# Thirty tiny loads in two groups in a single-token attention and MLP kernel

## The chip, the cores and the metric

The kernel runs on one core of one Trainium2 chip. The metric is the device time of one execution in microseconds. The kernel before was timed three times: 193.33, 193.45 and 193.55 us, median 193.45 us.

## The reference: what is computed

One token `x` (512 numbers) goes through a layer norm, and then through two branches.

```python
xn = _layernorm(x, axis=-1)
s = _A_ref(xn, A_k_cache, A_v_cache, A_wq, A_wo)   # attention
g = _silu(_B_ref(xn, B_w1, B_w2, B_w3, B_w4))      # MLP
return x + s * g
# in _A_ref: 32 heads of 128; the last W = 4096 of 32768 cached positions
q = x @ wq
scores = einsum(q, k) * 128 ** -0.5;  p = softmax(scores);  o = einsum(p, v) @ wo
# in _B_ref: x1 = x + shifted(h) @ w2;  h2 = gelu(layernorm(x1) @ w3) @ w4;  return x1 + h2
```

With one token, the four shifts of the MLP push all of `h` out, so `w1` is never needed, and the kernel multiplies `w2` with zeros. The bulk of the data is 32 heads x 4096 positions x 128 numbers of 2 bytes, once for K and once for V: 67 MB of the 79 MB that the kernel moves.

## The kernel before, in words

**Groups and stages.** The 32 heads are taken four at a time: eight groups, each with one K tile and one V tile of 4 MB (`load_kv`). The main loop (line 531) has ten passes `s`; in pass `s` the keys of group `s` are scored and the values of group `h = s - 2` are used. Below, K3 is the K tile of group 3, V0 the V tile of group 0. K0 comes in two transfers of 2 MB, K0a and K0b; V7 in three, V7a (2 MB), V7b and V7c (1 MB each). K has three buffers, V two. The two V buffers lie in the memory of the pool `wts`, which holds the weights `wq`, `w2`, `w3`, `w4` and what is made from them; the pool is closed in pass 2, so V0 is issued only once everything that reads this pool is done.

**Who does what.** For each group VectorE (DVE) multiplies a part of the keys with the query and sums along the row (`k_vector`, lines 321 and 323, in four parts); the other part is transposed on TensorE (PE), copied by ScalarE (ACT, line 342) and scored on PE (line 350). `sm_max`, `sm_turn`, `sm_exp`, `sm_den` and `sm_rden` make the softmax; `v_wide` (line 427) multiplies with the values. The query row is made on PE from `wq` (line 208); ACT and DVE copy it to `q_row` (lines 210, 211), ACT copies it once more (line 218), and spreads it over the partitions as `q_bc` (line 216), which every product of line 321 needs. Then ACT writes `q_pair` (line 225), which the scores on PE need.

**The order of the work.** From line 527 on, PE, DVE and ACT follow the order written out by hand in the loop. Ahead of it, a scheduler places the instructions. Loads go through two queues: SP issues the weights `w2`, `w3`, `w4` (its last 96 rows as a transfer of their own, "the tail of w4"), all K and V tiles, the `wo` tiles and the store, in the order of the program (`load`, line 75). ACT issues `x_bf`, `x_row` and `wq` (lines 79 to 84), in line with its other instructions.

**Completion counters.** A transfer raises a counter when it lands. In the built program there are eight of these counters, and they are handed out in turn, over both queues: `x_bf`, `w2`, `x_row`, `wq`, `w3`, `w4`, tail of `w4` and K0a take counters 0 to 7, K0b takes counter 0 again, K1 counter 1, K2 counter 2. A transfer that takes a counter over has a wait for the transfer that had it before: the built program lists K0b as waiting for `x_bf`, K1 for `w2` and K2 for `x_row`. These waits stand in the issuing engine's own order, so what is behind them on this engine waits as well.

Of the kernel before, what the change touches and what calls it, by code (L numbers as in the profile page):

```python
# [9 lines left out]
BF16 = mybir.dt.bfloat16  # L10
# [16 lines left out]
def kernel(  # L27
# [14 lines left out]
    nc = tc.nc  # L42
# [21 lines left out]
    small = ctx.enter_context(tc.tile_pool(name="small", bufs=1))  # L64
# [8 lines left out]
    wts = wts_guard.__enter__()  # L73

    def load(dst, src):
        return tc.keep_in_program_order(nc.sync.dma_start(out=dst, in_=src))  # L76
# [8 lines left out]
                        in_=A_wq.rearrange("(a b c) n -> b a (c n)", a=4, c=KC))  # L85
# [5 lines left out]
    load(w4_sb[:, 0:10, :], B_w4[0:10 * P, :].rearrange("(p c) n -> p c n", p=P))  # L91
    load(w4_sb[0:96, 10, :], B_w4[10 * P:F, :])


    def load_kv(pool, cache, g, cuts=(0, CP)):
        t = pool.tile([P, CP, Dh], BF16, tag="kv", name="kv")
        src = cache[0, G * g:G * g + G, W0:, :].rearrange("a (b c) d -> b a (c d)", b=PB)
        dst = t[:].rearrange("p c d -> p (c d)")
        for c0, c1 in zip(cuts, cuts[1:]):
            load(dst[:, c0 * Dh:c1 * Dh], src[:, :, c0 * Dh:c1 * Dh])  # L100
        return t
# [115 lines left out]
    for b in range(2):  # L217
# [5 lines left out]
        for t in range(2):  # L223
            rows = slice(64 * t, 64 * t + 64)
            nc.scalar.copy(out=q_pair[rows, 4 * b:4 * b + 4, :, G * t:G * t + G].rearrange("p g l a -> p g a l"),
                           in_=qt_ps[rows].bitcast(BF16).rearrange("p g (a m l) -> p g a m l", a=G, l=2)[:, :, :, 0, :])
# [38 lines left out]
    for i in range(11):  # L265
        n = P if i < 10 else 96
# [44 lines left out]
    def k_open(g):  # L311
        st[g] = {
            "sT": ps_s.tile([P, CP - 64, G], FP32, tag="sT", name="sT"),
            "S": sm_pool.tile([P, CP], FP32, tag="S", name="S"),
        }

    def k_vector(g, kn, part):
        m = nd(g) // 4
        rows = slice(m * part, m * part + m)
        prod = prod_pool.tile([P, 20, Dh], BF16, tag="prod", name="prod")  # L320
        nc.vector.tensor_tensor(out=prod[:, 0:m, :], in0=kn[:, rows, :],  # L321
                                in1=q_bc[:, g:g + 1, :].to_broadcast([P, m, Dh]), op=ALU.mult)
        nc.vector.tensor_reduce(out=st[g]["S"][:, rows], in_=prod[:, 0:m, :], axis=AX.X, op=ALU.add)  # L323
# [3 lines left out]
    def batches(g):  # L327
        n, m = nd(g), CP - nd(g)
        k = -(-m // 8)
        edges = [n + 2 * (m // 2 * i // k) for i in range(k + 1)]  # L330
        return list(zip(edges, edges[1:]))

    def k_turn(g, kn, b):
        c0, c1 = batches(g)[b]
        n = (c1 - c0) // 2
        pt = ps_tr.tile([P, 4, P], FP32, tag="pt", name="pt")
        for i in range(n):
            c = c0 + 2 * i
            nc.tensor.transpose(pt[:, i, :], kn[:, c:c + 2, :].rearrange("p c d -> p (c d)").bitcast(FP32),  # L339
                                ident_f[:])  # L340
        kts[b] = kt_pool.tile([P, 4, 2 * P], BF16, tag="kt", name="kt")
        nc.scalar.copy(out=kts[b][:, 0:n, :], in_=pt[:, 0:n, :].bitcast(BF16))  # L342

    def k_scores(g, b):
        kt = kts.pop(b)
        c0, c1 = batches(g)[b]
        for i in range((c1 - c0) // 2):
            c = c0 + 2 * i - nd(g)
            for l in range(2):
                nc.tensor.matmul(st[g]["sT"][:, c:c + 2, :].rearrange("p c a -> p (c a)"),  # L350
                                 lhsT=kt[:, i, l::2], rhs=q_pair[:, g, l, :], start=(l == 0), stop=(l == 1))
# [55 lines left out]
    def load_wo(i):  # L407
        h0, n = blocks[i]
        load(wo_blk[i], A_wo[h0 * P:(h0 + n) * P, :].rearrange("(p t) n -> p t n", p=P))
# [4 lines left out]
    def load_rows(h, n):  # L414
        load(wo_rows[:, h - h_part:h - h_part + n, :],
             A_wo[h * P:(h + n) * P, :].rearrange("(h p) n -> p h n", p=P))
# [18 lines left out]
    def v_turn(g):  # L435
        s = st[g]
        if g == NG - 1:
            ot_ps = ps_tr.tile([P, 4 * P], FP32, tag="pt", name="ot_ps")
        else:
            ot_ps = ps_misc.tile([P, 4 * P], FP32, tag="misc", name="ot_ps")  # L440
        s["ot"] = ot_ps
        step = P - 4
        for j in range(4):
            nc.tensor.transpose(ot_ps[:, step * j:step * j + P], s["ov_sb"][:, j, :], ident_f[:])  # L444
# [65 lines left out]
    def y_open():  # L510
        yr[0] = ps_tr.tile([P, KC, P], FP32, tag="pt", name="yr_ps")
        zeros(yr[0][:])
# [18 lines left out]
    for s in range(NG + LAG):  # L531
        h = s - LAG
        last = h == NG - 1
        kn = load_kv(k_pool, A_k_cache, s, (0, 64, CP) if s == 0 else (0, CP)) if s < NG else None
        if s == LAG:
            wts_guard.__exit__(None, None, None)
            v_pool = ctx.enter_context(tc.tile_pool(name="v", bufs=V_BUFS))
            wo_blk[2] = v_pool.tile([P, 4, D], BF16, tag="wo_4", bufs=1, name="wo_4")
            wo_rows = v_pool.tile([P, H - h_part, D], BF16, tag="wo_rows", bufs=1, name="wo_rows")
        if last:  # L540
            v = load_kv(v_pool, A_v_cache, h, cuts)
            for r in (H - G, H - 2):
                load_rows(r, 2)
        elif h >= 0:
            v = load_kv(v_pool, A_v_cache, h)
        if h == 3:
            wo_24 = k_pool.tile([P, 32, D], BF16, tag="kv", name="wo_24")
            wo_blk[0], wo_blk[1] = wo_24[:, 0:16, :], wo_24[:, 16:24, :]
            load_wo(0)
        if h == 5:  # L550
            load_wo(1)
            load_wo(2)

        if s < NG:
            nb = len(batches(s))

            def keys(b0, b1):
                for b in range(b0, b1):
                    k_turn(s, kn, b)
                    if b > 0:  # L560
                        k_scores(s, b - 1)

            k_open(s)
            k_vector(s, kn, 0)
            keys(0, 2)
            if s == 7:
                v_turn(h - 1)
                v_add(h - 1)
                v_out(h - 1)
            elif s > 1:  # L570
                sm_den(s - 2)
                sm_rden(s - 2)
            elif s == 1:
                sm_max(0)
            k_vector(s, kn, 1)
            keys(2, 4)
            if s == 7:
                sm_den(h)
                sm_rden(h)
                keys(4, nb - 2)  # L580
                sm_turn(s - 1)
                keys(nb - 2, nb)
            else:
                if s > 0:
                    sm_turn(s - 1)
                keys(4, nb)
            k_scores(s, nb - 1)
            sm_own(s)
            if s == 7:
                k_vector(s, kn, 2)  # L590
                v_wide(h, v)
                sm_exp(s - 1)
                v_turn(h)
                y_open()
                k_vector(s, kn, 3)
                v_add(h)
                v_out(h)
                ox_spread(1)
                sm_max(s)
                continue  # L600
            if s > 0:
                sm_exp(s - 1)
            if h > 0:
                v_turn(h - 1)
            k_vector(s, kn, 2)
            if h >= 0:
                v_wide(h, v)
            if h > 0:
                v_add(h - 1)
                v_out(h - 1)  # L610
            if s == 6:
                ox_spread(0)
            k_vector(s, kn, 3)
            if s == 6:
                ox_pick(0)
            if s > 0:
                sm_max(s)
        elif s == NG:
            ox_pick(1)
            sm_turn(NG - 1)  # L620
            sm_exp(NG - 1)
            y_wide(1, False)
            sm_den(NG - 2)
            sm_rden(NG - 2)
            y_wide(0, False)
            warm(3)
            v_wide(h, v)
            sm_den(NG - 1)
            sm_rden(NG - 1)
            v_turn(h)  # L630
            v_add(h)
            v_out(h)
            ox_spread(2)
        else:
            v_open(h)
            warm(3)
            v_wide(h, v, cuts[1], last=False)
            ox_pick(2)
            y_wide(2, True)
            nc.scalar.copy(out=y_sum[:], in_=yr[0][:].rearrange("p j n -> p (j n)"))  # L640
            v_wide(h, v, cuts[2], cuts[1])
            v_turn(h)
            v_add(h)
            rows_add(y_ps, ind, y_sum, False)
            v_part(h, v, cuts[2], CP)
            v_out(h)
            for r in range(H - G, H):
                y_head(r)
# [36 lines left out]
```

## Time and profile before

| | |
|---|---|
| median of three runs | 193.45 us |
| span of the profiled execution, first to last instruction | 191.2 us |
| around the span (the difference of the two; the page gives no separate time of the profiled execution) | 2.25 us |
| DVE busy | 150.9 us, 79% |
| PE busy / ACT busy | 116.4 us, 61% / 89.2 us, 47% |
| data moved | 79.02 MB, mean 413 GB/s |
| mean granted TensorE clock | 0.720 |

The span starts at 0 with the first instruction, and all times below are from there. "Queue" rows (SPq, ACTq) are the issuing of a transfer on SP or ACT: start, duration, what is loaded. A bracket at the end of a row is how long the engine sat idle before it and what ended that. The busy digits are tenths of 40 slices of the span.

### The profile page before, as it was taken

Reading aid. Unit: us, or ns where it says so; the run is one execution under the profiler, and the core shown is the slowest. Engines: PE = TensorE matmul, PEld = TensorE weight load, DVE = VectorE, ACT = ScalarE, POOL = GpSimd, SP = SyncE. Lnnn points to the kernel's source line nnn. Section 1 sums busy time; section 2 is a strip of 40 time slices with the busy share of each in tenths; the row PEclk is TensorE's granted clock in tenths of the full one; section 3 lists DMA queues with packets and bytes.
Section 4 is the critical chain, followed back from the end, with each engine's and each line's share of the span. In section 5 each row is a group of like instructions: output and inputs, shape, how many; then the busy total and the mean of one; then the engine's idle time right before and its main releaser. Section 6 shows DMA issues by size and latency. Waiting matters only on the chain.

```text
span 191.2 us, 2839 instructions
## 1 busy us (share of the span) xinstructions
PE 116.4 (61%) x1159; PEld 74.2 (39%) x1159; DVE 150.9 (79%) x175; ACT 89.2 (47%) x191; POOL 2.3 (1%) x11
## 2 busy tenths in 40 slices
PE   1653754989825368256845772680888189739762
PEld 0430222767614334143334441540763077313322
DVE  1660159979999999999999999999999999980111
ACT  2001370888794076427464564542475148733120
POOL 2110000000000000000000000000000000000000
PEclk9999695555755557955695588557567858975998
DMA  6999999999999999999999999999999998999990
GB/s 211 447 430 404 431 418 439 439 439 437 432 434 439 432 429 432 432 439 432 422 432 432 418 422 418 452 439 435 439 432 434 435 432 372 471 425 405 420 371 32
DMA packets 4572, 79.02 MB, mean 413 GB/s; under 512 B 624, under 2 KB 1232, under 8 KB 1488
## 3 DMA queue, kind: packets, MB, share of 16 engines
q1 hardware_dynamic: 4264, 74.65, 91.6%
q10 hardware_dynamic: 296, 4.20, 5.1%
q8 instruction: 9, 0.15, 0.3%
q14 instruction: 3, 0.02, 0.0%
HBM read 78.84 MB, written 0.00 MB: 412 GB/s over the span
## 4 chain that ended last, share of the span: by engine, by line
DVE 46%; DMA 43%; PE 5%; ACT 3%; issue 1%; SPq 1%; ACTq 0%; DVEq 0%
DMA kv<-in_A_k_cache_dram 31%; DVE S L323 28%; DVE prod L321 15%; DMA kv<-in_A_v_cache_dram 10%; ACT kt L342 3%; DMA x_bf<-in_A_x_dram 2%; PE pt L339 2%; PE ov L427 1%; DVE m L366 1%; DVE S L364 1%; SPq L76 1%; PE sT L350 1%; DVE mx L374 1%; PE oT L461 1%; PE ot_ps L444 0%
## 5 line engine op out<-in xcount | busy, mean ns | idle before, releaser
L323 DVE TENSOR_REDUCE S<-prod 128x20 f32<-128x2560 bf16 (+1 forms) x32 | 86.0, 2686 | 1.1
L342 ACT COPY kt<-pt 128x1024 bf16<-128x1024 bf16 x52 | 51.2, 1013 | 40.4 <-PE pt L339 38.7
L339 PE MATMUL pt<-ident_f,kv 128*128 128x128 f32 x208 | 46.7, 376 | 10.8 <-DMA kv<-in_A_k_cache_dram 10.8
L321 DVE TENSOR_TENSOR prod<-kv,q_bc 128x2560 bf16<-128x2560 bf16 (+1 forms) x32 | 45.4, 1418 | 3.9 <-DMA kv<-in_A_k_cache_dram 3.7
L339 PEld LDWEIGHTS pt<-ident_f,kv 128*128 128x128 f32 x208 | 34.2, 196 | 14.4 <-DMA kv<-in_A_k_cache_dram 10.5
L350 PE MATMUL sT<-q_pair,kt 128*128 128x8 bf16 x416 | 19.4, 170 | 15.7 <-ACT kt L342 15.5
L350 PEld LDWEIGHTS <-kt 128*128 128x128 bf16 x416 | 16.4, 104 | 26.8 <-ACT kt L342 25.8
L427 PE MATMUL ov<-kv,pT 128*16 128x512 bf16 x248 | 22.0, 515 | 1.4 <-DMA kv<-in_A_v_cache_dram 1.4
L388 ACT ACTIVATE pT<-S,mb 128x128 bf16<-128x128 f32 x32 | 13.9, 573 | 0.3
L372 PE MATMUL mt_ps<-ident_f,m 128*1 128x128 f32 x8 | 2.9, 359 | 17.4 <-DVE rden L399 16.9
L433 ACT COPY ov_sb<-ov 128x512 f32<-128x512 f32 x8 | 4.7, 586 | 17.1 <-PE ov L427 17.1
L427 PEld LDWEIGHTS <-pT 128*16 128x16 bf16 x248 | 6.9, 109 | 13.2 <-issue 11.4
L359 ACT ACTIVATE own<-sT,par 128x48 f32<-128x48 f32 (+1 forms) x32 | 7.5, 356 | 3.7 <-PE sT L350 3.7
L444 PE MATMUL ot_ps<-ident_f,ov_sb 128*128 128x128 f32 x32 | 7.1, 359 | 2.9 <-ACT mb L384 1.9
L211 DVE CAST q_row<-qr_ps 128x512 bf16<-128x512 f32 x1 | 0.7, 692 | 9.9 <-PE qr_ps L208 9.9
L388 ACT ACTIVATION_READ_ACCUMULATOR pT<-S,mb 128x1 f32 x32 | 8.3, 258 | 0.0
L372 PEld LDWEIGHTS mt_ps<-ident_f,m 128*1 128x1 f32 x8 | 0.6, 80 | 17.9 <-DVE rden L399 17.2
L399 DVE RECIPROCAL rden<-den_ps 128x4 f32<-128x4 f32 x8 | 1.4, 175 | 7.0 <-PE den_ps L394 7.0
L381 PE MATMUL mb_ps<-md,par_t 5*128 5x4 f32 x16 | 3.9, 311 | 4.1 <-DVE md L376 4.1
L255 ACT ACTIVATE a_row<-a_ps 128x384 bf16<-128x384 f32 x1 | 0.5, 491 | 12.0 <-remote 12.0
L444 PEld LDWEIGHTS ot_ps<-ident_f,ov_sb 128*128 128x128 f32 x32 | 4.5, 178 | 3.9 <-ACT mb L384 2.3
L208 PE MATMUL qr_ps<-wq_sb,xq_bf 128*1 128x512 bf16 x32 | 3.1, 566 | 3.7 <-DMA wq_sb<-in_A_wq_dram 3.7
(122 smaller groups left out, 81.6 us busy)
## 6 DMA issues: line engine op xcount, KB each, us to landing
kv<-in_A_k_cache_dram SPq DMA_DIRECT2D x7, 4096.0 KB, 31.3
kv<-in_A_v_cache_dram SPq DMA_DIRECT2D x7, 4096.0 KB, 30.6
wq_sb<-in_A_wq_dram ACTq DMA_DIRECT2D x1, 4096.0 KB, 17.6
kv<-in_A_k_cache_dram SPq DMA_DIRECT2D x2, 2048.0 KB, 27.4
wo<-in_A_wo_dram SPq DMA_DIRECT2D x1, 2048.0 KB
kv<-in_A_v_cache_dram SPq DMA_DIRECT2D x1, 2048.0 KB
kv<-in_A_v_cache_dram SPq DMA_DIRECT2D x2, 1024.0 KB, 17.6
w_sb<-in_B_w_dram SPq DMA_DIRECT2D x1, 1376.0 KB, 9.1
```

The lines of the kernel that those rows point to most:

```text
L321: nc.vector.tensor_tensor(out=prod[:, 0:m, :], in0=kn[:, rows, :], in1=q_bc[:, g:g + 1, :].to_broadcast([P, m, Dh]), op=ALU.mult)
L323: nc.vector.tensor_reduce(out=st[g]["S"][:, rows], in_=prod[:, 0:m, :], axis=AX.X, op=ALU.add)
L339: nc.tensor.transpose(pt[:, i, :], kn[:, c:c + 2, :].rearrange("p c d -> p (c d)").bitcast(FP32), ident_f[:])
L342: nc.scalar.copy(out=kts[b][:, 0:n, :], in_=pt[:, 0:n, :].bitcast(BF16))
L350: nc.tensor.matmul(st[g]["sT"][:, c:c + 2, :].rearrange("p c a -> p (c a)"), lhsT=kt[:, i, l::2], rhs=q_pair[:, g, l, :], start=(l == 0), ...
L359: nc.scalar.mul(s["own"][:, 0:m, a], s["sT"][:, 0:m, a], par[:, a:a + 1])
L372: nc.tensor.transpose(mt_ps[:], s["m1"][:], ident_f[:])
L381: nc.tensor.matmul(mb_ps[:], lhsT=par_t[:].rearrange("k b a -> k (b a)"), rhs=md[:], start=True, stop=True)
L388: nc.scalar.activation(out=s["pT"][:, :, a], in_=s["S"][:], func=ACT.Exp, scale=scale, bias=mb[:, a:a + 1], accum_out=s["sum"][:, a:a + 1])
L427: nc.tensor.matmul(ov[r:r + 4 * G], lhsT=s["pT"][:, c:c + 4, :].rearrange("p i a -> p (i a)"), rhs=v[:, c:c + 4, :], start=(i < 4), stop=( ...
L433: nc.scalar.copy(out=s["ov_sb"][:], in_=ov[:])
L444: nc.tensor.transpose(ot_ps[:, step * j:step * j + P], s["ov_sb"][:, j, :], ident_f[:])
```

## The change

A helper `marks` issues fifteen loads of 1 to 15 rows of 5 to 19 numbers (10 to 38 bytes a row) from `B_w2` into a small tile that nothing reads. It is called twice: on ACT right behind the issue of `wq`, into a tile in the pool `wts`, and on SP in pass 2, behind the issue of K2 and ahead of V0, into a tile in the pool `small`. No computation changes.

```diff
+    tags = small.tile([16, 180], BF16, name="tags")
+    tags_a = wts.tile([16, 180], BF16, name="tags_a")
+
+    def marks(queue, t):
+        c = 0
+        for k in range(1, 16):
+            n = 4 + k
+            tc.keep_in_program_order(queue.dma_start(out=t[0:k, c:c + n], in_=B_w2[16 * k:17 * k, 0:n]))
+            c += n
+
+    marks(nc.scalar, tags_a)
...
         kn = load_kv(k_pool, A_k_cache, s, (0, 64, CP) if s == 0 else (0, CP)) if s < NG else None
+        if s == 2:
+            marks(nc.sync, tags)
         if s == LAG:
             wts_guard.__exit__(None, None, None)
```

Below, A1 to A15 are the fifteen loads on ACT and S1 to S15 those on SP.

## The prediction

> **What bounds the kernel now.** I read the page first, then SP's waits and issues, then the rows where an engine waited for a transfer.
>
> ```profile
> span 191.2 us, 2839 instructions
> DMA  6999999999999999999999999999999998999990
> ```
> ```profile
> 0.00:4.80 4.80, 0.61 (x1) 0.10 (x1) 0.60 (x7) 1.28 (x1) 1.23 (x9) 1.00 0.66 210
> 4.80:24.00 19.20, 10.99 (x86) 5.31 (x87) 6.68 (x39) 2.27 (x5) 1.11 (x2) 0.91 1.01 430
> 42.00:130.00 88.00, 53.26 (x539) 36.21 (x536) 86.94 (x66) 50.23 (x115) 0.00 (x0) 0.65 1.01 433
> 130.00:168.00 38.00, 25.32 (x256) 17.71 (x256) 36.40 (x35) 20.07 (x42) 0.00 (x0) 0.73 1.00 428
> ```
>
> The last two figures of a stretch are the DMA share and GB/s; the DVE's busy time is the third after the length. The DMA engines are full (1.00, about 430 GB/s) from start to end, so a gap in their work is lost for good. From 42 to 130 us DVE is busy for 86.94 of 88 us as well. So there are two bounds, and they run level: a delay of either reaches the end once the slack between them is used.
>
> ```profile
> 4.71 1.18 SPq L76 DMA_DIRECT2D kv<-in_A_k_cache_dram  x2
> 6.83 0.54 SPq L76 DMA_DIRECT2D kv<-in_A_k_cache_dram  x1
> 31.19 0.53 SPq L76 DMA_DIRECT2D kv<-in_A_v_cache_dram  x1
> ```
> ```profile
> SPq L76 <- DMA x_bf<-in_A_x_dram: 1.4, 1, 1.4
> SPq L76 <- DMA x_row<-in_A_x_dram: 0.9, 1, 0.9
> ```
> ```profile
> kv<-in_A_k_cache_dram SPq DMA_DIRECT2D x1, 4096.0 KB, 36.5
> ```
> ```profile
> kv<-in_A_v_cache_dram SPq DMA_DIRECT2D x1, 4096.0 KB, 30.1
> ```
>
> SP issues K0b and K1 at 4.71 us, K2 at 6.83 us, V0 at 31.19 us. K0b and K2 use neither `x_bf` nor `x_row`, yet SP waited for these: that is the counter taken over, at work. The last two lines are the issues of K1 (5.29 us) and V0 with their times to landing: they land at 41.8 and 61.3 us, and K2, half way between, at about 51.6 us. V0 is queued 20 us before the DMA engines reach it; that is SP's slack.
>
> ```profile
> 2.96 1.28 ACT L255 ACT_TABLE_LOAD   x1 [2.96 <-issue]
> 21.84 0.59 ACT L210 CAST q_row<-qr_ps 128x512 bf16<-128x512 f32 x1 [5.13 <-PE qr_ps L208]
> 26.09 1.23 DVE L321 TENSOR_TENSOR prod<-kv,q_bc 128x2048 bf16<-128x2048 bf16 x1 [2.19 <-DMA kv<-in_A_k_cache_dram]
> 41.91 1.49 DVE L321 TENSOR_TENSOR prod<-kv,q_bc 128x2560 bf16<-128x2560 bf16 x1 [0.99 <-DMA kv<-in_A_k_cache_dram]
> 134.17 1.49 DVE L321 TENSOR_TENSOR prod<-kv,q_bc 128x2560 bf16<-128x2560 bf16 x1 [0.55 <-DMA kv<-in_A_k_cache_dram]
> ```
> ```profile
> 181.50 1.04 PE L427 MATMUL ov<-kv,pT 128*16 128x512 bf16 x16 [1.02 <-DMA kv<-in_A_v_cache_dram]
> 183.93 0.61 PE L427 MATMUL ov<-kv,pT 128*16 128x512 bf16 x8 [0.41 <-DMA kv<-in_A_v_cache_dram]
> 186.38 0.96 PE L461 MATMUL oT<-pT,kv 128*128 128x4 bf16 x32 [0.17 <-DMA kv<-in_A_v_cache_dram]
> ```
>
> These are the few places where computing waited for data: all its slack is 0.99 + 0.55 us on DVE and 1.02 + 0.41 + 0.17 us on PE at the end.
>
> **The change, part by part.** The bytes are nothing: 30 loads of at most 15 rows of 38 bytes. What counts is where they wait. The built program of the changed kernel hands the eight counters on through the new loads, and lists these waits. On ACT: A4 waits for `wq`, A6 for `w4`, A7 for K0a, A8 to A13 for A1 to A6, A14 for K0b, A15 for A7. On SP: K0b waits for the tail of `w4`, K1 for A8, K2 for A9, S1 to S6 for A10 to A15, S7 for K1, S8 for K2, S9 to S15 for S1 to S7, V0 for S8, K3 for S9. Behind ACT's loads stands all its computing, behind SP's all later tiles.
>
> *The price of one issue.* No load of few rows stands on SP; the nearest rows are these (issues of 128, 4 and 4 partitions):
>
> ```profile
> 0.74 0.40 ACTq L79 DMA_DIRECT2D x_bf<-in_A_x_dram  x1
> 1.18 1.11 ACTq L82 DMA_DIRECT2D x_row<-in_A_x_dram  x1
> ```
> ```profile
> 188.68 0.66 SPq L76 DMA_DIRECT2D out_dram<-out_row  x1
> ```
>
> So 0.40 to 1.11 us each; I take 0.66, of few rows and on SP. Issue to first data: in the first 4.80 us the DMA share is 0.66, so the engines begin at 4.80 x 0.34 = 1.6 us, 0.9 us after the first issue at 0.73 us; I take 1.0, and 1.5 as the upper end for queues that are busy.
>
> *ACT.* K0b is issued at 21.2 us (the tail of `w4` lands 19.1 us after its issue at 2.11) in place of 4.71. K0a lands at 26.0, so the engines still have work queued then, and K0b lands as before, 27.4 us after 4.71: at 32.1. A14 goes then, A15 after it: 2 x 0.66, to 33.4 us. The table load (1.28), which ACT did at 2.96 us while it had nothing to do, is now behind this: 34.7. The built order then has one copy to `q_row` (0.59), two copies within it (0.62 each) and the first `q_bc` (0.59): 37.1. So the first product on DVE starts at 37.2 instead of 26.1, 11.1 us late. Its waits at 41.91 and 134.17 go, since the keys are then early: 11.1 - 0.99 - 0.55 = 9.6. In the new order `g_row` and `bv` come later, between the products; DVE may wait for `h_ps` there, 0 to 0.6 us; I take 0.2: 9.8. The softmax of group 7 hangs on DVE (`m`, then `mt_ps`, `mb_ps`, `pT`), so PE gets to V7 9.8 us later and saves the three waits, 1.6 us. **Computing would end 8.2 us later.** Bounds: with issues of 0.40 and no wait 7.5, with 1.11 and 0.6 us of wait 9.5.
>
> *The transfers.* First gap, before K1: A7 and A8 are issued from 26.0 to 27.3 us, A8 lands some 2 to 4 us on (`x_bf`'s 4.0 from issue to landing is the nearest row), K1 is issued at 29.3 to 31.3 and brings data 1.0 later, while the slowest DMA engine is done with K0b shortly before 32.1: 0 to 1.5 us, I take 0.4. Second gap, before V0: K2 now lands at 52.0; only then S8 goes, with S9 to S15 behind it on SP: 8 x 0.66 = 5.3, V0's own wait for S8 is over by then; V0's data comes 1.0 later. The engines stand idle 6.3 us. K3 and V1 follow at once, as K0's buffer is free at 52. **The transfers would end 6.7 us later.** Bounds: 0 + 8 x 0.40 + 1.0 = 4.2 and 1.5 + 8 x 1.11 + 1.5 = 11.9 us. Later issues wait for buffers that computing frees, 10 us late; they keep a queue ahead of them, since K6 (issued at 112.0 us) had 12 us and V7 9 us of other transfers before it, and the difference between the two delays is some 3 us. S1 to S7 cost nothing more: SP has until K2 lands.
>
> *Sum.* The later of the two ends counts: 8.2 us. Span 191.2 + 8.2 = 199.4; with the 2.25 us around it 201.65, and 193.45 + 8.2 gives the same for the median.
>
> *A rule weighed.* The Trainium skill, in "DMA: Bandwidth & Descriptors", section "Anatomy of one DMA", gives a DMA a fixed cost of about 2.0 us however small it is. Were each of the eight loads after K2 charged that in series, the second gap would be an estimated 8 x 2.0 + 1.0 = 17 us and the kernel 17.4 us slower. The rows above speak against it: SP goes on after 0.66 us, and V0 waits only for S8's landing, under cover of the seven issues behind it.
>
> **The rivals.**
> - *The transfers bind after all, cheaply.* The delay on DVE is taken up by something that I don't see (PE idles 4.73 us for K7 at 153.5, which shows slack on PE and ACT, though not on DVE). Then the end goes by the second gap: 6 to 6.7 us, 199.5 to 200.2 us. Against it: DVE had only 1.5 us of waits from 26 to 154 us.
> - *Issues are dear.* At `x_row`'s 1.11 us the second gap is 8 x 1.11 + 1.0 = 9.9, with the first 10.3 to 11.9: 203.8 to 205.3 us. Then the DMA binds. It decides from about 0.85 us an issue (0.4 + 8 x 0.85 + 1.0 = 8.2).
> - *The loads are hidden; not slower.* SP does nothing from 7.4 to 31.19 us and ACT nothing from 4.2 to 16.2. Were the loads free to go when reached, 15 x 0.66 = 9.9 us would fit into both, and the time would stay 193.45. It decides if V0 is issued before about 50 us and ACT free before 21.8. Against it stand SP's waits for `x_bf` and `x_row`, which show that a counter taken over is waited for.
>
> **How the numbers follow.** The forecast (8.2, computing binds, 200.7 to 203) has 0.5, the cheap rival 0.2, dear issues 0.18, hidden loads 0.03, the rest lies outside on either side: both delays below 6 us (0.04), or a third stall (0.05). The predicted time is 201.6 us. The range 199.3 to 204.8 us takes in the cheap rival, all of computing's bounds and the lower part of dear issues. About 0.2% (0.4 us) is what a measurement of this kernel can tell from no change. Slower by more: 0.96; within it: 0.03, the hidden loads; faster: 0.01.
>
> **What would show it.** ACT: first copy to `q_row` near 34.7 us, behind a table load that starts after 33 us; first product of DVE near 37.2. SP: K1 issued near 30 us, S8 at about 52, V0 near 57.4. DMA digits: one slice near 52 to 58 us almost empty, and a small dip near 31. No waits of DVE for keys at K1 and K6, and PE waits at the end smaller than before. Wrong it would be if V0 is issued well before K2 lands (then nothing hangs on the counters), if an issue is far from 0.66 us, or if DVE catches up between 42 and 150 us, which its row of 86.94 in 88 us excludes as far as I see.

## The result, and the profile after

The changed kernel takes 204.56 us (median of four runs, 204.15 to 204.81) beside 193.50 us for the kernel before (193.33 to 193.63): a ratio of 1.0567, 95% interval 1.0551 to 1.0582 (intervals below are the same kind). The profiled execution took 204.41 us and has a span of 202.2 us. The kernel is 11.06 us slower. The forecast was 201.6 us, its range 199.3 to 204.8. Three of the twelve executions of e11, below, took 196.1 to 196.4 us, a slower state of the same kernel, and its figures leave them out.

Lines of the kernel after stand 12 further down than before from the helper on (321 is 333, 427 is 439), and 14 further down behind the second call. First the span and the DMA digits of the page after:

```profile
span 202.2 us, 2871 instructions
DMA  6999995999239999999999999999999999999990
```

One slice is 5.06 us. There is a dip in slice 7 (30 to 35 us) and a hole in slices 11 and 12 (50 to 61 us), where the page before has nothing but nines. The next two fences give the same stretches of both kernels, before and then after, as in the prediction: the DVE's busy time is the third after the length, the last two figures are the DMA share and GB/s.

```profile
20.00:40.00 20.00, 14.41 (x136) 8.73 (x134) 14.51 (x12) 11.00 (x17) 0.00 (x0) 0.67 1.04 443
40.00:62.00 22.00, 14.43 (x149) 11.68 (x147) 20.73 (x16) 17.05 (x31) 0.00 (x0) 0.58 1.00 429
```
```profile
20.00:40.00 20.00, 7.88 (x62) 3.94 (x62) 5.37 (x5) 8.04 (x14) 0.00 (x0) 0.66 0.90 370
40.00:62.00 22.00, 15.02 (x186) 11.04 (x183) 20.64 (x17) 15.95 (x25) 0.00 (x0) 0.74 0.70 289
29.50:32.50 3.00, 0.00 (x0) 0.00 (x0) 0.00 (x0) 0.64 (x1) 0.00 (x0) 0.50 0.18 61
52.20:59.00 6.80, 5.18 (x53) 4.17 (x50) 6.70 (x6) 3.77 (x5) 0.00 (x0) 0.50 0.04 9
```

What the first stretch did not move is (443 - 370) x 20 us, at 430 GB/s 3.4 us of transfers; what the second did not move is (429 - 289) x 22 us, 7.2 us. The lower two rows show where: the engines stand still around 31 us, and from 52.2 to 59.0 us. Together this is 10.6 of the 11.06 us. Such a sum hangs on where the window ends and is rough: for the run e2 below, 274 GB/s from 40 to 62 us gives 7.9 us where 7.3 were lost.

The rows of SP after (start, duration, what is loaded) show who kept them waiting: K0b, K1 with K2 behind it, S7, S8 to S15 in one row, V0. `tags` and `tags_a` are the tiles of the tiny loads.

```profile
31.22 1.18 SPq L76 DMA_DIRECT2D kv<-in_A_k_cache_dram  x2
44.92 0.27 SPq L102 DMA_DIRECT2D tags<-in_B_w_dram  x1
54.63 2.97 SPq L102 DMA_DIRECT2D tags<-in_B_w_dram  x8
57.78 0.55 SPq L76 DMA_DIRECT2D kv<-in_A_v_cache_dram  x1
```

And SP's waits after (total us, times, longest):

```profile
SPq L76 <- DMA tags_a<-in_B_w_dram: 9.4, 1, 9.4
SPq L102 <- DMA kv<-in_A_k_cache_dram: 17.7, 2, 9.4
```

K1, a 4 MB transfer, stood 9.4 us behind A8, a load of eight rows of 24 bytes, and all of S7 to V0 stood behind the landings of K1 and K2. V0 is issued at 57.78 us in place of 31.19.

Computing after, at the rows that answer to those of before:

```profile
31.86 1.28 ACT L222 ACT_TABLE_LOAD   x1 [31.86 <-DMA tags_a<-in_B_w_dram]
```
```profile
35.29 1.23 DVE L333 TENSOR_TENSOR prod<-kv,q_bc 128x2048 bf16<-128x2048 bf16 x1 [11.00 <-ACT q_bc L228]
45.23 0.29 DVE L290 TENSOR_TENSOR bv<-xn_row,h_ps 128x128 f32<-128x128 f32 x1 [1.08 <-PE h_ps L167]
51.33 1.49 DVE L333 TENSOR_TENSOR prod<-kv,q_bc 128x2560 bf16<-128x2560 bf16 x1
144.52 1.49 DVE L333 TENSOR_TENSOR prod<-kv,q_bc 128x2560 bf16<-128x2560 bf16 x1 [1.49 <-DMA kv<-in_A_k_cache_dram]
```
```profile
192.07 1.04 PE L439 MATMUL ov<-kv,pT 128*16 128x512 bf16 x16 [0.81 <-DMA kv<-in_A_v_cache_dram]
194.56 0.61 PE L439 MATMUL ov<-kv,pT 128*16 128x512 bf16 x8 [0.47 <-DMA kv<-in_A_v_cache_dram]
197.08 1.00 PE L473 MATMUL oT<-pT,kv 128*128 128x4 bf16 x32 [0.24 <-DMA kv<-in_A_v_cache_dram]
```

DVE starts 9.2 us late and does its first product of K1 9.4 us late (51.33 against 41.91). At K6 it waits for the keys, 1.49 us where it waited 0.55 before, and is then 10.35 us late; the three waits for V7 at the end are still there, 10.6 to 10.7 us late. So the last wait is for a transfer everywhere: the transfers bind, and computing follows them with about 1.5 us to spare (0.81 + 0.47 + 0.24 at the end).

### The profile page after: what moved, and what is told of

Read it like the earlier page. It is cut to its first block, busy times and chain, and to the rows that moved or that the text cites. A ratio compares the mean times of both kernels' runs of the same rounds, so it can differ in the third digit from the quotient of the medians.

```text
span 202.2 us, 2871 instructions
## 1 busy us (share of the span) xinstructions
PE 118.1 (58%) x1159; PEld 74.3 (37%) x1159; DVE 151.0 (75%) x175; ACT 90.1 (45%) x192; POOL 2.3 (1%) x11
## 4 chain that ended last, share of the span: by engine, by line
DVE 47%; DMA 35%; PE 7%; ACT 7%; SPq 1%; issue 1%; ACTq 1%
DVE S L335 29%; DMA kv<-in_A_k_cache_dram 24%; DVE prod L333 15%; DMA kv<-in_A_v_cache_dram 9%; ACT kt L354 3%; PE pt L351 2%; DMA tags_a<-in_B_w_dram 2%; SPq L76 1%; PE sT L362 1%; ACTq L102 1%; PE ov L439 1%; DVE m L378 1%; DVE S L376 1%; ACT L267 1%; ACT L222 1%
## 5 line engine op out<-in xcount | busy, mean ns | idle before, releaser
L351 PE MATMUL pt<-ident_f,kv 128*128 128x128 f32 x208 | 44.7, 362 | 9.3 <-DMA kv<-in_A_k_cache_dram 9.3
L351 PEld LDWEIGHTS pt<-ident_f,kv 128*128 128x128 f32 x208 | 32.9, 189 | 13.2 <-DMA kv<-in_A_k_cache_dram 10.6
L439 PE MATMUL ov<-kv,pT 128*16 128x512 bf16 x248 | 22.9, 530 | 1.3 <-DMA kv<-in_A_v_cache_dram 1.3
L226 PE MATMUL qb_ps<-q_row,sel 128*128 128x512 bf16 x2 | 1.0, 606 | 10.2 <-ACT q_row L222 10.2
```

The lines of the kernel that those rows point to most:

```text
L439: nc.tensor.matmul(ov[r:r + 4 * G], lhsT=s["pT"][:, c:c + 4, :].rearrange("p i a -> p (i a)"), rhs=v[:, c:c + 4, :], start=(i < 4), stop=( ...
```

## The experiments

Three theories stood at first. **W**: the loads cost only by what their place in the turn of the eight counters makes wait (two gaps). **C**: computing, late behind ACT, sets the end. **P**: each tiny load costs the DMA engines themselves about 0.37 us (11 us over 30). Later came **A** (the reserved tiles, by moving other buffers, cost the rest) against **L** (the loads cost it). Every edit starts from the changed kernel unless it says otherwise; where loads are left out, all that is computed stays. The kernel before was timed again beside them, with medians of 193.40 to 193.48 us; ratios are against these.

### One group alone

e1 leaves out the group on SP, e2 the group on ACT.

```diff
 # e1
-        if s == 2:
-            marks(nc.sync, tags)
 # e2
-    marks(nc.scalar, tags_a)
```

> Three theories. W (gaps in the transfers, by the waits on counters): the 11.1 us are two gaps, 2.9 us before K1 (K1 waits for A8) and 7.5 us before V0 (S8 waits for K2, and seven more issues follow), and the later start of computing (+9.4 us at K1) is hidden under them. C (computing): ACT, held until 31.9 us, delays DVE, and that alone makes the time. P (packets): each tiny load costs the DMA engines or the queues a fixed share, 11.06 / 30 = 0.37 us, wherever it stands. With the fifteen loads on ACT alone: W has one gap of 2.9 us left, so computing binds, 9.4 less 0.55 us at K6 and 1.6 us at the end = +7.3, 200.8 us, and DVE should not wait at K6; C expects the full 204.5 us; P expects 193.5 + 5.5 = 199.0 us.

> The fifteen loads on SP alone. W: the gap before V0 alone, +6.5 to +7.5 us, 200.0 to 201.0 us, with V0 issued about 3.2 us after S8, and S8 when K2 has landed (51.6 us). C: ACT is free, no change, 193.5 us. P: 193.5 + 5.5 = 199.0 us.

e2 took 201.41 us (201.19 to 201.53), ratio 1.0402, interval 1.0381 to 1.0423: the second gap alone is most of the loss. Its SP rows and one window:

```profile
51.76 3.10 SPq L102 DMA_DIRECT2D tags<-in_B_w_dram  x8
55.04 0.55 SPq L76 DMA_DIRECT2D kv<-in_A_v_cache_dram  x1
```
```profile
49.20:56.00 6.80, 4.75 (x41) 3.74 (x39) 6.73 (x5) 5.70 (x16) 0.00 (x0) 0.50 0.06 16
```

The engines are empty from about 49.2 us, SP sees K2's landing at 51.76, the eight loads take until 55.04, V0's data comes at about 56: 2.6 + 3.3 + 1.0 = 6.8 us.

e1 took 202.61 us (201.97 to 204.73), ratio 1.0487, interval 1.0428 to 1.0546, between W's and C's figures. Here computing does set the end: no wait for keys or values is left after the first product, and the DMA digits run out before the end.

```profile
DMA  6999995999999999999999999999999999959900
```
```profile
35.36 1.23 DVE L333 TENSOR_TENSOR prod<-kv,q_bc 128x2048 bf16<-128x2048 bf16 x1 [11.12 <-ACT q_bc L228]
46.65 0.29 DVE L290 TENSOR_TENSOR bv<-xn_row,h_ps 128x128 f32<-128x128 f32 x1 [1.86 <-PE h_ps L167]
52.75 1.49 DVE L333 TENSOR_TENSOR prod<-kv,q_bc 128x2560 bf16<-128x2560 bf16 x1
```

So the delay of computing is by itself worth 202.61 - 193.44 = 9.2 us (with the tiles in place), and only the larger delay of the transfers hides it in the changed kernel. The first gap of the transfers is in e1 too, hidden behind that delay. The profiled execution of e1 was its slowest (204.73 us); from 170 to 202 us PE was granted 0.66 of its clock in it, against 0.82 in the kernel after. But over the whole execution its clock, 0.692, does not stand out from the other three (0.679 to 0.695), so why e1's times spread stays open.

### How many loads on SP

e3 has six loads on SP, e4 eight, both none on ACT. With six, V0 takes over K1's counter and K3 takes K2's; with eight, S7 takes K1's and S8 takes K2's, and V0 stands right behind S8.

```diff
-    marks(nc.scalar, tags_a)
-        for k in range(1, 16):
+        for k in range(1, 7):     # e3;  range(1, 9) in e4
```

> Only six loads on SP (S1 to S6), none on ACT. By the built program S6 waits for K0b, V0 for K1 (41.8 us) and K3 for K2 (51.6 us), each while another 4 MB is queued. W: no gap, 193.5 us. P: 6 x 0.37 = 2.2, 195.7 us. C: 193.5 us.

> Eight loads on SP (S1 to S8), none on ACT: two more than in the run with six. S8 now waits for K2 to land, and V0 stands right behind it. W: a step, S8's issue 0.35, V0's data 1.2 us later and the landing of K2 seen late by some 1 to 2 us: +3.5 to +4.5 us, 197.0 to 198.0 us; and from here to fifteen loads 0.4 us per load. P: 8 x 0.37 = 3.0, 196.5 us, 0.75 us above six loads. C: 193.5 us.

e3 took 194.24 us (194.23 to 194.44), ratio 1.0040, interval 1.0025 to 1.0056, V0 is issued at 42.18 us, when K1 has landed, and K2's 4 MB are still to move. e4 took 198.75 us (198.41 to 198.97), ratio 1.0267, interval 1.0247 to 1.0287. Two loads more, of seven and eight rows, cost 198.75 - 194.24 = 4.5 us; the seven behind them cost 201.41 - 198.75 = 2.66 us, 0.38 each. That step is what P cannot give. SP's issue of V0 in e3, then e4's rows and a window of e4:

```profile
42.18 0.54 SPq L76 DMA_DIRECT2D kv<-in_A_v_cache_dram  x1
```
```profile
51.94 0.27 SPq L102 DMA_DIRECT2D tags<-in_B_w_dram  x1
52.39 0.54 SPq L76 DMA_DIRECT2D kv<-in_A_v_cache_dram  x1
```
```profile
49.20:53.00 3.80, 3.02 (x34) 2.41 (x32) 3.77 (x4) 2.74 (x6) 0.00 (x0) 0.50 0.08 28
```

Even one load that waits for K2 leaves the engines empty for 3.8 us: V0 was held until K2 had landed, and the queue behind K2 was empty.

### One load fewer on ACT

e6 has 13 loads on ACT, e8 12; SP keeps its fifteen. With 13, K1 takes over K0b's own counter and goes only when K0b has landed; with 12 it takes A6's, and K2 takes K0b's. ACT is free 3 us sooner in both (table load at 28.74 and 28.61 us).

```diff
-    def marks(queue, t):
+    def marks(queue, t, top=15):
-        for k in range(1, 16):
+        for k in range(1, top + 1):
-    marks(nc.scalar, tags_a)
+    marks(nc.scalar, tags_a, 13)     # e6;  12 in e8
```

> Thirteen loads on ACT (A14 and A15 gone), fifteen on SP. ACT is free after A13, some 3.6 us sooner than in the changed kernel, and by the built program K1 now waits for K0b itself, so the gap before K1 stays. W (the two gaps in the transfers set the end): about the time of the changed kernel, 203.7 to 204.6 us. C (the late start of computing sets it): 3.6 us less, 201 us. P (each tiny load costs 0.37 us): 193.5 + 28 x 0.37 = 203.9 us.

> Twelve loads on ACT, one less than in the run with thirteen, fifteen on SP. By the built program K1 now waits for A6 (issued near 21 us) and K2 for K0b. W: K1 is issued near 27 us, the gap before it is gone and only that before V0 is left, as with SP's loads alone: 201.4 us, some 2.5 us less than with thirteen. C: no difference from thirteen, 201 us for both. P: 193.5 + 27 x 0.37 = 203.5 us, 0.4 us less than with thirteen.

e6 took 204.69 us (204.27 to 205.00), ratio 1.0578, interval 1.0558 to 1.0597; e8 201.84 us (201.65 to 202.06), ratio 1.0432, interval 1.0417 to 1.0448. SP's issue of K1 with K2, first e6, then e8:

```profile
31.26 1.18 SPq L76 DMA_DIRECT2D kv<-in_A_k_cache_dram  x2
```
```profile
26.98 4.75 SPq L76 DMA_DIRECT2D kv<-in_A_k_cache_dram  x2
```

and DVE in e6:

```profile
32.17 1.22 DVE L333 TENSOR_TENSOR prod<-kv,q_bc 128x2048 bf16<-128x2048 bf16 x1 [7.88 <-ACT q_bc L228]
144.75 1.49 DVE L333 TENSOR_TENSOR prod<-kv,q_bc 128x2560 bf16<-128x2560 bf16 x1 [3.03 <-DMA kv<-in_A_k_cache_dram]
```

In e6 computing starts 3.1 us sooner than in the changed kernel and gains nothing; DVE only waits longer for K6. That refutes C for the changed kernel. One load fewer, and the first gap is gone: from 29.5 to 32.5 us the DMA share is 0.22 in e6 and 1.02 in e8, in this order:

```profile
29.50:32.50 3.00, 1.72 (x6) 0.84 (x6) 0.33 (x1) 2.99 (x6) 0.00 (x0) 0.50 0.22 83
```
```profile
29.50:32.50 3.00, 1.84 (x6) 0.97 (x6) 0.46 (x1) 2.98 (x6) 0.00 (x0) 0.50 1.02 432
```

The first gap is worth 204.69 - 201.84 = 2.85 us; the changed kernel less e2 gives 3.15.

### The same loads without the waits

e5 issues all thirty on the POOL engine (the first group behind the layer norm), whose transfers have counters of their own in the built program. e7 has six loads on ACT and none on SP.

```diff
 # e5
-    marks(nc.scalar, tags_a)
+    marks(nc.gpsimd, tags_a)      # ahead of xn_row
-            marks(nc.sync, tags)
+            marks(nc.gpsimd, tags)
```

> All thirty loads, moved to POOL's queue behind its last computing instruction. In the built program POOL's transfers take eight counters of their own, so K0b, K1 and K2 wait as in the kernel before, and ACT and SP have nothing in line; V0 alone waits for the fifteen loads into the pool wts too. W and C: 193.5 us, at most 0.8 us more (what six loads on SP cost). P: 193.5 + 11.1 = 204.6 us.

> Six loads on ACT (A1 to A6), none on SP. A6 waits for w4 (20.9 us), so ACT is free near 21.3 us, about when it got its first copy in the kernel before (21.84), with the table load of 1.28 us behind it; K1 waits for K0a (26 us) while K0b is still queued. W: no gap, and computing starts up to 1 us late, which the 0.99 us wait for K1 takes up: 193.5 to 194.5 us. C: the same. P: 195.7 us.

e5 took 194.57 us (194.41 to 194.86), ratio 1.0053, interval 1.0037 to 1.0070, and V0, which by the built program waits for the fifteen loads into the pool `wts`, is issued at 33.97 us, well before K2 has landed:

```profile
33.97 0.54 SPq L76 DMA_DIRECT2D kv<-in_A_v_cache_dram  x1
```

e7 took 194.25 us (194.08 to 194.38), ratio 1.0039, interval 1.0026 to 1.0052. P asked for 204.6 and 195.7 and falls: thirty such loads are nearly free where no large transfer waits for them so long that the engines run out of work. W asked for no change in e3 and allowed up to 194.3 us in e5 and 194.5 in e7; but that all three stand 0.4 to 0.5% above the kernel before pointed to something that it lacked.

### The rest: the tiles alone

e9 keeps both tiles and issues no load; e10 is e9 with the first tile 256 numbers wide instead of 180. The first shifts the buffers behind it by 384 bytes a partition, the second by 512. e11 is the kernel before with the K buffers (and `kt` and `prod` behind them) shifted by 128 bytes, which puts K on a multiple of 256, and the rest by 512. e12 is the changed kernel with the tile of e10.

```diff
 # e9
-    marks(nc.scalar, tags_a)
-            marks(nc.sync, tags)
 # e10: also;  e12: this alone
-    tags = small.tile([16, 180], BF16, name="tags")
+    tags = small.tile([16, 256], BF16, name="tags")
 # e11, on the kernel before, ahead of the K buffers
+    lead = ctx.enter_context(tc.tile_pool(name="lead", bufs=1))
+    lead.tile([P, 64], BF16, name="lead")
...
-    small.tile([P, 96], BF16, name="pad")
+    small.tile([P, 288], BF16, name="pad")
```

> The two small tiles are reserved as in the change, but no load is issued. All three runs without a gap (six loads on SP, six on ACT, thirty on POOL) stand 0.8 to 1.1 us above the kernel before. Theory A (addresses): the tile in the pool small takes 384 bytes a partition and moves what lies behind it, the weights and both V buffers among it, by 384 bytes; that costs 0.8 us, so here 194.2 us too. Theory L (loads): the loads themselves cost it; here 193.4 us.

> As the run with the tiles alone, but the tile in small is 256 numbers wide, so everything behind it moves by 512 bytes in place of 384. If A holds and it is the place within 512 bytes that matters: 193.4 us. If any move costs: 194.2 us. L: 193.4 us.

> The kernel before with a pad of 128 bytes a partition ahead of the K buffers and the pad behind them widened by 384: the K buffers begin at 256 within 512 bytes, as the V buffers do, in place of 128; the V buffers and the weights keep their place within 512. If the place within 512 bytes costs K what it cost V and the weights (0.65 us): 192.8 us. If K's transfers don't mind, or if what was seen came from another tile: 193.4 us.

> The changed kernel with all thirty loads where they are, the tile in small 256 numbers wide, so that everything behind moves by 512 bytes more than the loads' own tile in wts, in place of 384. If the addresses' share adds to the two gaps: 204.56 - 0.65 = 203.9 us. If it is hidden under the gaps: 204.5 us.

| run | median us | ratio | interval |
|---|---|---|---|
| e9, tiles, no loads | 194.10 | 1.0034 | 1.0022 to 1.0046 |
| e10, shift of 512 bytes | 193.43 | 0.9995 | 0.9986 to 1.0005 |
| e11, K at 256 | 193.19 | 0.9990 | 0.9977 to 1.0003 |
| e12, all loads, shift of 512 | 203.79 | 1.0529 | 1.0510 to 1.0549 |

e9 costs as much as e3 and e7 with their loads: A holds, L falls; what e5 has beyond it (1.0053 against 1.0034) is no more than the two intervals allow, which overlap. The tile takes 0.34%, 0.65 us, by where it puts the other buffers, and 0.77 us of the changed kernel goes with it in e12. In the built program the V buffers start 256 bytes past a multiple of 512 before, and 128 past it after a shift of 384. The Trainium skill, in "DMA: Bandwidth & Descriptors", section "How a descriptor splits into AXI transactions", says that a transaction of a descriptor must start on a multiple of 256 bytes: where the descriptor starts elsewhere, its first transaction begins at the multiple below it, and the bytes before its start "are fetched but unused and still cost beats". It speaks of bytes fetched, while the buffers moved here are those that the loads write. e9 and e10 go the way of such a rule (0.65 us and none). e11 does not: the K buffers, moved from 128 onto 256, gained nothing that can be measured.

The traces tell a part of which buffers matter. DVE's first product of K1 waits for K1's landing in all these kernels; it starts at 41.91 us in the kernel before, and in e9, e10 and e3, in this order:

```profile
42.22 1.49 DVE L332 TENSOR_TENSOR prod<-kv,q_bc 128x2560 bf16<-128x2560 bf16 x1 [1.09 <-DMA kv<-in_A_k_cache_dram]
```
```profile
41.87 1.49 DVE L332 TENSOR_TENSOR prod<-kv,q_bc 128x2560 bf16<-128x2560 bf16 x1 [1.10 <-DMA kv<-in_A_k_cache_dram]
```
```profile
42.20 1.49 DVE L332 TENSOR_TENSOR prod<-kv,q_bc 128x2560 bf16<-128x2560 bf16 x1 [1.15 <-DMA kv<-in_A_k_cache_dram]
```

With the shift of 384 bytes K1 lands 0.3 us later, and in e3 V0 is issued only at 42.18 us. So about half of the cost is there before any V tile is moved, when of the large shifted buffers only the weights have been loaded. The products themselves are not slower (1484 ns on average before and in e9). Where the other half falls was not separated, and the mechanism stays open.

## Why the prediction was right and wrong, by its steps

**The account.** In us: addresses 0.65 (e9), second gap 201.41 - 193.44 - 0.65 = 7.3 (e2), first gap 2.85 (e6 and e8): 10.8 of 11.06 measured. With 3.15 for the first gap, which is the changed kernel less e2, the sum closes by construction.

**Right: where the cost sits.** The waits on counters came as read from the built program, both gaps lie where they were put, and K2 landed as forecast (51.76 us in e2, which has no first gap; forecast 52.0); in the changed kernel S8 went at 54.63, later by the larger first gap. V0 was issued at 57.78 us, forecast 57.4, though by two errors that cancelled: a first gap 2.6 us larger and issues 2.2 us cheaper. The rival of hidden loads fell.

**Luck in the number.** 204.56 us lies above the 200.7 to 203 of the forecast's own mechanism (whose lower bound of 7.5 us gives 200.95, not 200.7). It is inside the stated range only in the part that was put there for dear issues, and issues were cheap. Two of the named signs came out against the forecast: DVE still waited for keys at K6 (1.49 us), and an issue was far from 0.66 us.

**Wrong: "computing ends 8.2 us later" as the bound.** As a delay it was nearly right: 9.2 us in e1. In the parts, ACT was free at 31.86 us (forecast 33.4) and DVE began at 35.29 (forecast 37.2), both earlier; but the wait for `h_ps`, taken at 0.2 with 0.6 as its end, measured 1.08 us after and 1.86 in e1, with another 0.48 for `hr_ps`. The transfers were the larger of the two, 11.06 us against the forecast's 6.7, and the later end counts.

**Wrong: the first gap, 0.4 us taken, about 3 measured.** K1 went at 31.22 us, the late end of the 29.3 to 31.3 that were forecast. The error is at the other edge: the term "the slowest engine is done shortly before 32.1" took K0b's landing for the time when the engines run dry. K0b had landed by 31.07, a microsecond sooner than forecast, when A14, which waits for it, was issued; and the engines had run dry a microsecond earlier:

```profile
30.00:31.00 1.00, 0.00 (x0) 0.00 (x0) 0.00 (x0) 0.00 (x0) 0.00 (x0) 0.50 0.08 2
```

A8 was issued at 26.49 and released SP at 31.22, 4.7 us later and just after K0b's landing. Its eight short rows were issued while K0b's 2 MB were under way; that they had to wait for these is argued, not shown.

**Wrong: the second gap, 6.3 us taken, 7.3 paid.** The issue price of 0.66 us was too high: issues took 0.25 to 0.40 us on ACT and 0.27 to 0.50 on SP, and e4 to e2 gives 0.38 each, so eight are 3.1 to 3.3 us, not 5.3. In return the idle time begins 2.6 us before K2's landing is seen (e2: engines empty at 49.2, landing at 51.76), a term that the sum lacked; it made the gap start at the landing. The Trainium skill, in "DMA: Bandwidth & Descriptors", section "Why a DMA increments its semaphore by 16 and not by 1", says that a transfer has landed only when the last of its engines is done; e4's share of 0.08 while the landing was still out agrees, though no view here shows a single engine. About 0.5 us lies outside the empty stretch of 6.8 us; it was not settled further.

**Wrong: no cost for the tiles.** 0.65 us, which the prediction didn't look for.

**The rivals.** "Issues are dear" gave 203.8 to 205.3 us, where the time came out, and for the wrong reason: issues were cheaper than taken. That the transfers bind was right in it. The reading that was weighed, 2.0 us for each load in series, falls: eight loads went out in 2.97 us. The Trainium skill, in "DMA: Bandwidth & Descriptors", section "Anatomy of one DMA", gives the figure for loads that GpSimd issues; these stand on SP.

## What to carry to other kernels

Where counters are handed out in turn, read from the built program who takes over whose counter before adding even a tiny transfer: its price is the time by which it holds the next large one on its queue, here two gaps of 3 and 7 us, and nearly nothing for the same loads on a queue with other counters. Begin a gap where the engines run dry, not where the last transfer is seen to land, and end it where the next data flows. When two bounds run level, work out both delays with the same care, since the larger one hides the other.

## What the runs showed of the hardware

- A load of eight rows of 24 bytes took 4.7 us from issue to release while K0b's 2 MB were under way; the tiny loads of e5 on POOL's queue took 5.4 to 18.1 us to land, and their issue on POOL 0.52 us each.
- A 4 MB transfer was seen to land 2.6 to 2.7 us after the engines' share had dropped to near nothing (0.08 from 49.2 to 53.0 us in e2 and e4).
- A tile that nothing uses cost 0.65 us by shifting other buffers by 384 bytes, and nothing by 512 bytes (e9, e10).
